# The first eight rows of x loaded by SyncE without a cast, and a kernel's prologue dealt out anew over the engines

## The chip, the cores and the metric

The kernel runs on one core of one Trainium2 chip. The metric is the time of one execution on the device in microseconds (us), as the median of several runs. The engines are named as in the profile: PE is TensorE, DVE is VectorE, ACT is ScalarE, POOL is GpSimd, SP is SyncE. In every trace of this case each of them works through its own instructions in the order of the program, and that order is what this study is about.

## The reference, cut to what matters

```python
def _attn_ref(x):                        # x: 8 x 3008 x 256, float32
    X = np.fft.fft(x, axis=1)
    X = np.fft.fft(X, axis=2)
    return X.real.astype(np.float32)

def _moe_ref(x, w_gate, w_val, w_out):   # 24064 tokens, 256 -> 1536 -> 256
    gate = np.maximum(x @ w_gate, 0.0)
    val = x @ w_val
    return (gate * val @ w_out).astype(np.float32)
```

The kernel does the Fourier transforms as matmuls with tables of cosines and sines, which it makes on the chip, and folds the last step of the transform into the two weight matrices. So before the main loop can start, a prologue has to load the first batch of x and the weights, make the tables, run the first transform stage, and fold the weights. The main loop begins with the first matmul into a tile called `G`.

## The kernel before: the parts that the change touches

GpSimd loads the first batch in pieces; the loads cast float32 to bfloat16 on the way. Rows 0 to 15 land in a tile `lo`, rows 16 to 31 in `hi` (through an index, in turned order).

```python
def load_first(r, n):
    # ... cut: makes the tile lo or hi at the first use
    if r < NB // 2:
        nc.gpsimd.dma_start(out=dst, in_=view(x, r * D, [[NB * D, 96], [1, n * D]]))
    else:
        # ... cut: indirect load of the same size on GpSimd

def ends(r, n):       # VectorE, a few columns
def back(r, n, evac): # a copy of the rows in reversed order, on ScalarE or VectorE
```

The weights come in halves of 128 rows; a pair is added and subtracted, and TensorE folds the sum and the difference with a cosine (`cs` 0) or sine table. The fold is in float32, on 64 columns of the array for each half.

```python
def pair_w(n, i, eng, parts=(0, 1)):
    lo, hi, up = (wst[i, n, c] for c in range(3))
    if 0 in parts: eng.tensor_tensor(up, lo, hi, op=ALU.add)         # L323
    if 1 in parts: eng.tensor_tensor(lo, lo, hi, op=ALU.subtract)    # L325

def fold_w(n, i, cs, ps=None):
    for k, w in ((0, wst[i, n, 2]), (1, wst[i, n, 0])):
        nc.tensor.matmul(ps[64 * k:64 * k + 64, :], lhsT=cd[:, cs, 64 * k:64 * k + 64], rhs=w, ...)  # L335
```

GpSimd's order before (cuts marked); the schedule is manual, so program order is the order on each engine:

```python
load_first(0, 8)
# ... cut: iotas for the row index ixf
load_first(24, 8); pl.iota(pi[:], ...); load_first(8, 4); load_first(20, 4)
# ... cut: two iotas
load_first(12, 4); load_first(16, 4)
pl.tensor_scalar(perm[:], dd[:], ...)
# ... cut: three iotas
load_w(0, pl)                            # four loads of the first weights
# tis: two 128x128 steps that need small columns from VectorE
# ... cut: di, s, rot
pair_w(0, 1, pl)                         # sum and difference of the value weights
```

VectorE makes the tables, the reversed copies, seven small column operations (`col`, 128x1 each), a masking step on `tis`, and then `pair_w(0, 0, dve)` for the gate weights. TensorE then runs: first stage, gate folds, two "upright" groups, value folds, first `G`.

## Time and profile before

| of the kernel before | value |
|---|---|
| time, median of 3 runs | 623.52 us (623.28 to 623.77) |
| span of the profiled run | 622.2 us |
| first matmul into G | 21.87 us |
| span after that point | 600.3 us |
| GpSimd's value sum begins, its difference ends | 16.43, 19.18 us |
| VectorE's gate sum begins | 15.12 us |
| TensorE's granted clock in the prologue | 1.00 |

Of 622 us, the change touches only the first 22. The prediction below shows the lines; a line of a timeline gives start, length, engine, source line, operation, tiles and shapes, and in brackets the idle time before it and what ended it.

### The profile page before, as it was taken

The page shows a single profiled execution, that of the slowest core. Times are in us where ns is not written, and L with a number is a line of the kernel's source. Part 1 is how long each engine was busy: PE and PEld are TensorE (multiplying, and loading weights), DVE is VectorE, ACT ScalarE, POOL GpSimd, SP SyncE. Part 2 cuts the span into 40 slices and gives each one's busy share as a digit, 9 for nine tenths or more (in the row PEclk, how much of TensorE's full clock was granted, in tenths as well). Part 3 has the DMA queues.
Part 4 walks back from the last instruction along what each step waited for, and adds up shares of the span by engine and source line. Part 5 has one row for each costly group of instructions (what it writes and reads, how often), then busy time and mean ns, then how long its engine had stood idle before and what let it go on. Part 6 is the DMA issues. An engine that isn't in the chain of part 4 may idle for free.

```text
span 622.2 us, 11959 instructions
## 1 busy us (share of the span) xinstructions
PE 613.3 (99%) x4284; PEld 409.1 (66%) x4284; DVE 537.0 (86%) x652; ACT 444.9 (72%) x855; POOL 519.9 (84%) x447
## 2 busy tenths in 40 slices
PE   8999999999999999999999999999999999999996
PEld 5346666666666666666667666666666666666665
DVE  7678998899888898898988998898988888899991
ACT  7677777777777777767777777767677676766661
POOL 8998998998898898899988998888988965555665
PEclk9999999999999999999999999999999999999998
DMA  8994283425462182613843255531822134112114
GB/s 168 243 166 111 84 217 89 112 66 177 111 154 61 47 220 87 149 36 95 211 107 89 67 164 123 141 75 34 234 71 58 34 85 125 52 34 67 34 35 100
DMA packets 42038, 67.44 MB, mean 108 GB/s; under 512 B 5877, under 2 KB 31774, under 8 KB 39962
## 3 DMA queue, kind: packets, MB, share of 16 engines
q1 hardware_dynamic: 37162, 50.61, 31.5%
q0 software_dynamic: 4656, 15.88, 10.8%
q8 instruction: 33, 0.54, 0.4%
q10 hardware_dynamic: 160, 0.20, 0.1%
q14 instruction: 27, 0.22, 0.1%
HBM read 38.85 MB, written 30.17 MB: 111 GB/s over the span
## 4 chain that ended last, share of the span: by engine, by line
PE 96%; DMA 1%; POOL 1%; DVE 1%; issue 0%; ACT 0%; POOLq 0%
PE po L686 40%; PE V L636 20%; PE G L620 10%; PE G L621 10%; PE G L627 10%; PE psw L335 2%; PE ps L164 2%; PE ps L273 2%; DMA lo<-in_x_dram 1%; POOL hi L133 0%; PE pst L242 0%; PE ps L218 0%; PE ps L168 0%; DVE E L643 0%; POOL lo L130 0%
## 5 line engine op out<-in xcount | busy, mean ns | idle before, releaser
L657 POOL TENSOR_TENSOR h<-gm,E 128x992 bf16<-128x992 f32 (+1 forms) x138 | 319.9, 2318 | 82.0 <-DVE E L664 52.9
L686 PE MATMUL po<-wo,h 128*128 128x256 bf16 (+2 forms) x2304 | 328.5, 272 | 0.0
L686 PEld LDWEIGHTS <-h 128*128 128x128 bf16 (+2 forms) x2304 | 231.3, 103 | 106.0 <-issue 0.2
L629 ACT ACTIVATE gm<-G 128x496 f32<-128x496 f32 (+1 forms) x288 | 170.4, 592 | 94.4 <-PE G L627 87.2
L650 DVE TENSOR_TENSOR h<-gs,V 128x1024 bf16<-128x1024 f32 (+3 forms) x150 | 173.8, 1159 | 62.1 <-PE V L636 42.1
L643 DVE SCALAR_TENSOR_TENSOR E<-nb,af,V 128x496 f32<-128x496 bf16 (+1 forms) x276 | 190.1, 730 | 1.1 <-PE V L636 0.7
L622 ACT ACTIVATE gs<-G 128x497 f32<-128x497 f32 (+2 forms) x288 | 169.7, 589 | 24.6 <-PE G L621 24.4
L664 DVE SCALAR_TENSOR_TENSOR E<-E,V 128x992 f32<-128x992 f32 (+1 forms) x138 | 164.3, 1191 | 0.0
L620 PE MATMUL G<-pq,wc 128*128 128x497 bf16 (+2 forms) x288 | 108.0, 375 | 0.0
L621 PE MATMUL G<-pq,ws 128*128 128x497 bf16 (+2 forms) x288 | 108.0, 375 | 0.0
L627 PE MATMUL G<-pq,wm 128*128 128x496 bf16 (+1 forms) x288 | 107.9, 375 | 0.0
L636 PE MATMUL V<-pq,wc 128*128 128x497 bf16 (+2 forms) x288 | 85.5, 375 | 0.3 <-DVE h L657 0.3
L636 PE MATMUL V<-pq,ws 128*128 128x497 bf16 (+2 forms) x288 | 85.4, 375 | 0.2 <-DVE E L643 0.2
L621 PEld LDWEIGHTS <-ws 128*128 128x128 bf16 x288 | 28.2, 98 | 31.6
L699 ACT COPY os<-po 128x512 f32<-128x512 f32 x63 | 36.9, 586 | 14.3 <-PE po L686 12.0
L620 PEld LDWEIGHTS <-wc 128*128 128x128 bf16 x288 | 28.2, 98 | 20.1 <-issue 1.6
L115 POOL TENSOR_TENSOR eo<-xla 94x256 bf16<-94x256 f32 x56 | 40.5, 730 | 0.6
L636 PEld LDWEIGHTS <-wc 128*128 128x128 bf16 x288 | 28.2, 98 | 19.0 <-issue 0.5
L115 POOL TENSOR_TENSOR eo<-xlb 94x256 bf16<-94x256 f32 (+1 forms) x42 | 34.4, 820 | 0.7
L112 POOL TENSOR_TENSOR xla<-xla,xha 94x510 f32<-94x510 f32 x28 | 32.9, 1174 | 2.2
L179 ACT CAST t<-ps 96x512 bf16<-96x512 f32 x56 | 32.7, 584 | 2.3 <-PE ps L164 0.2
L627 PEld LDWEIGHTS <-wm 128*128 128x128 bf16 x288 | 28.1, 98 | 3.8
(140 smaller groups left out, 366.2 us busy)
## 6 DMA issues: line engine op xcount, KB each, us to landing
out_dram<-os SPq DMA_DIRECT2D x124, 128.0 KB
Td<-t SPq DMA_DIRECT2D x7, 768.0 KB
t<-Td SPq DMA_DIRECT2D x7, 768.0 KB
out_dram<-os SPq DMA_DIRECT2D x82, 64.0 KB
xla<-in_x_dram SPq DMA_DIRECT2D x7, 720.0 KB
xlb<-in_x_dram SPq DMA_DIRECT2D x6, 640.0 KB
nb<-Nd SPq DMA_DIRECT2D x23, 128.0 KB
out_dram<-os SPq DMA_DIRECT2D x40, 48.0 KB
```

The lines of the kernel that those rows point to most:

```text
L115: yield eng.tensor_tensor(e1[:, :, k:k + H], x1[:, :, 0:H], free(x1, D, [DX, n], [-1, H]), op=op)
L620: nc.tensor.matmul(G[:, ds], lhsT=wc[0][:, fs], rhs=pq[:, 0, ds], start=True, stop=False)
L621: nc.tensor.matmul(G[:, ds], lhsT=ws[0][:, fs], rhs=pq[:, 1, ds], start=False, stop=True)
L622: nc.scalar.activation(pair(t, "gs")[:, t % 2, ds], G[:, ds], ACTF.Relu)
L627: nc.tensor.matmul(G[:, cols], lhsT=wm[0][:, f * 128:(f + 1) * 128], rhs=pqt[b, blk][:, 1, cols], start=False, stop=True, skip_group_check ...
L629: nc.scalar.activation(pair(t, "gm")[:, t % 2, cols], G[:, cols], ACTF.Relu)
L636: nc.tensor.matmul(o, lhsT=w[:, f * 128:(f + 1) * 128], rhs=pqt[b, blk][:, min(k, 1), cs], start=(k == 0), stop=(k > 0 or split(t)), skip_ ...
L643: nc.vector.scalar_tensor_tensor(pair(t, "E")[:, t % 2, cols], nbt[b, blk][:, cols], af[:, f:f + 1], pair(t, "V")[:, t % 2, cols], op0=ALU ...
L650: nc.vector.tensor_tensor(pair(t, "h")[:, k, 0, 0:ds.stop - ds.start], pair(t, "gs")[:, k, ds], val, op=ALU.mult)
L657: eng.tensor_tensor(free(pair(t, "h")[:], 1024 * (t % 2) + 512 + w - 1, [1024, n], [-1, w]), pair(t, "gm")[:, k, cols], val[:, :, cols], o ...
L664: nc.vector.scalar_tensor_tensor(E[:, :, cols], E[:, :, cols], 2.0, V[:, :, cols], op0=ALU.mult, op1=ALU.subtract)
L686: nc.tensor.matmul(po[0:m, i, :], lhsT=pair(t - f + ff, "h")[:, ff % 2, sg, g * 128:g * 128 + m], rhs=wo[:, ff, :], start=(ff == 0), stop= ...
```

## The change

Its intent: SyncE is idle at the start and can issue a load at once, but in this kernel only GpSimd issues casting loads. So SyncE loads rows 0 to 7 as float32 into a tile of batch 1 that is not used yet (`x8`), and copies on GpSimd cast them into `lo`, which the first matmuls read. That frees one issue on GpSimd and lets the stream of transfers begin sooner. VectorE's reversed copies read `x8` directly; two new copies on GpSimd (the "casts") make rows 0 to 7 of `lo`. Small work is dealt out otherwise: the columns to GpSimd, one negation from ScalarE to VectorE, one evacuation from VectorE to ScalarE, perm and some iotas behind the weight loads.

```diff
+        x8 = tabs["x8"] = x_tile(False, 0)
+        nc.sync.dma_start(out=x8[:, 0:8, :], in_=view(x, 0, [[NB * D, 96], [1, 8 * D]]))
 ...
-        load_first(0, 8)
 ...
         load_first(8, 4)
+        pl.tensor_copy(xt[0]["lo"][0:NA, 2:8, 0:H], x8[0:NA, 2:8, 0:H])      # 1st cast
         load_first(20, 4)
 ...
-        pl.tensor_scalar(perm[:], dd[:], ...)
+        pl.iota(pi[:], ...)
+        pl.tensor_copy(xt[0]["lo"][0:NA, 0:2, 0:H], x8[0:NA, 0:2, 0:H])      # 2nd cast
+        load_w(0, pl)
         # ... three iotas
-        load_w(0, pl)
 ...
         def col(tag, a, *args, **kw):
-            dve.tensor_scalar(t[:], a[:], *args, **kw)
+            pl.tensor_scalar(t[:], a[:], *args, **kw)
 ...
-        warm(9)
+        warm(4)
-        nc.scalar.mul(wn[:, 0, 9:16, :], wn[:, 1, 9:16, :], -1.0)
+        dve.tensor_scalar(wn[:, 0, 9:16, :], wn[:, 1, 9:16, :], scalar1=-1.0, ...)
 ...     # VectorE's angle, bits and table steps for cd stand later
+        pl.tensor_scalar(perm[:], dd[:], ...)
 ...
+        dve.tensor_scalar(tis[:], tis[:], scalar1=NB - 1, ..., op0=ALU.bitwise_and)
         pair_w(0, 0, dve)
-        first_evac(0, "dve")
+        first_evac(0, "act")
```

More of the change, by code (lines that the diff above doesn't have):

```diff
@@ L185, in ends @@
     def ends(r, n):
-        v = xt[0]["lo" if r < NB // 2 else "hi"][0:NA, r % 16:r % 16 + n, :]
+        v = (tabs["x8"] if r < 8 else xt[0]["lo" if r < NB // 2 else "hi"])[0:NA, r % 16:r % 16 + n, :]
         if r < NB // 2:
@@ L196, in back @@
         dst = tabs["back"][:, r:r + n, 1:H]
-        src = free(xt[0]["lo" if r < NB // 2 else "hi"][0:NA], r % 16 * D + D - 1, [D, n], [-1, H - 1])
+        src = free((tabs["x8"] if r < 8 else xt[0]["lo" if r < NB // 2 else "hi"])[0:NA], r % 16 * D + D - 1, [D, n], [-1, H - 1])
         if evac == "act":
@@ L409 @@
         load_first(24, 8)
-        pl.iota(pi[:], pattern=[[0, 1]], base=0, channel_multiplier=1)
         load_first(8, 4)
+        pl.tensor_copy(xt[0]["lo"][0:NA, 2:8, 0:H], x8[0:NA, 2:8, 0:H])
         load_first(20, 4)
@@ L416 @@
         load_first(16, 4)
-        pl.tensor_scalar(perm[:], dd[:], scalar1=mi[:], scalar2=None, op0=ALU.is_equal)
+        pl.iota(pi[:], pattern=[[0, 1]], base=0, channel_multiplier=1)
+        pl.tensor_copy(xt[0]["lo"][0:NA, 0:2, 0:H], x8[0:NA, 0:2, 0:H])
+        load_w(0, pl)
         iota(pl, ui[:], [[1, 4], [0, NB]], 0, 0)
@@ L466 @@
             sines(free(wz[:], 192 * (k + 1), [97, 2], [2, 48]), both[0], S, 2.0 * k - 1.0)
-        nc.scalar.mul(wn[:, 0, 9:16, :], wn[:, 1, 9:16, :], -1.0)
-        back(0, 2, "dve")
-        dve.tensor_scalar(da[:], dd[:], scalar1=mi[:], scalar2=None, op0=ALU.mult)
-        residue(da[:], dq[:], D, dve)
-        absolute(dq[:], da[:])
-        cosines(cd[:, 0, 1:H], dq[:, 1:H], D)
-        sines(cd[:, 1, 1:H], da[:, 1:H], D, 1.0)
-        jj, sl, up, odd = bits(0, 15), bits(4, 1), bits(5, 3), bits(0, 1)
+        dve.tensor_scalar(wn[:, 0, 9:16, :], wn[:, 1, 9:16, :], scalar1=-1.0, scalar2=None, op0=ALU.mult)
         ends(24, 8)
@@ L483 @@
         back(8, 4, "act")
+        dve.tensor_scalar(da[:], dd[:], scalar1=mi[:], scalar2=None, op0=ALU.mult)
+        residue(da[:], dq[:], D, dve)
         for c in (1, 2, 3):
             first_evac(c, "act")
+        absolute(dq[:], da[:])
+        cosines(cd[:, 0, 1:H], dq[:, 1:H], D)
+        sines(cd[:, 1, 1:H], da[:, 1:H], D, 1.0)
+        jj, sl, up, odd = bits(0, 15), bits(4, 1), bits(5, 3), bits(0, 1)
         z = col("z", jj, scalar1=0.0, scalar2=None, op0=ALU.is_equal)
@@ L498 @@
             pl.tensor_scalar(ti[cs], kbi[:], scalar1=mul[:], scalar2=(o0, o1)[cs][:], op0=ALU.mult, op1=ALU.add)
-        dve.tensor_scalar(tabs["wzn"][:], wz[:, 0], scalar1=-1.0, scalar2=None, op0=ALU.mult)
-        dve.tensor_copy(cd[:, 1, 0:1], odd[:])
-        dve.tensor_scalar(cd[:, 0, 0:1], odd[:], scalar1=-1.0, scalar2=1.0, op0=ALU.mult, op1=ALU.add)
-        dve.tensor_scalar(ui[:], ui[:], scalar1=up[:], scalar2=-1.0, op0=ALU.is_equal, op1=ALU.mult)
         group((4, 5), False)
@@ L508 @@
         group((4, 5), True)
+        dve.tensor_scalar(tabs["wzn"][:], wz[:, 0], scalar1=-1.0, scalar2=None, op0=ALU.mult)
+        back(0, 2, "dve")
         ends(12, 4)
@@ L512 @@
         back(16, 4, "dve")
-        dve.tensor_scalar(tis[:], tis[:], scalar1=NB - 1, scalar2=None, op0=ALU.bitwise_and)
+        dve.tensor_copy(cd[:, 1, 0:1], odd[:])
+        dve.tensor_scalar(cd[:, 0, 0:1], odd[:], scalar1=-1.0, scalar2=1.0, op0=ALU.mult, op1=ALU.add)
+        dve.tensor_scalar(ui[:], ui[:], scalar1=up[:], scalar2=-1.0, op0=ALU.is_equal, op1=ALU.mult)
+        pl.tensor_scalar(perm[:], dd[:], scalar1=mi[:], scalar2=None, op0=ALU.is_equal)
         group((6, 7, 0), False)
@@ L520 @@
         first_evac(5, "act")
+        dve.tensor_scalar(tis[:], tis[:], scalar1=NB - 1, scalar2=None, op0=ALU.bitwise_and)
         pair_w(0, 0, dve)
-        for cs in range(2):
-            nc.scalar.activation(sv[cs][:], ti[cs], ACTF.Sin, scale=2.0 * math.pi / NB * (1.0 - 2e-7), bias=npi[:])
         group((6, 7, 0), True)
@@ L526 @@
         first_evac(7, "act")
-        first_evac(0, "dve")
+        first_evac(0, "act")
+        for cs in range(2):
+            nc.scalar.activation(sv[cs][:], ti[cs], ACTF.Sin, scale=2.0 * math.pi / NB * (1.0 - 2e-7), bias=npi[:])
         for cs in range(2):
```

## The prediction

> **What bounds the kernel now.** I read the page first: busy shares, then the chain that ended last.
>
> ```profile
> span 622.2 us, 11959 instructions
> PE 613.3 (99%) x4284; PEld 409.1 (66%) x4284; DVE 537.0 (86%) x652; ACT 444.9 (72%) x855; POOL 519.9 (84%) x447
> PE 96%; DMA 1%; POOL 1%; DVE 1%; issue 0%; ACT 0%; POOLq 0%
> ```
>
> TensorE is the bound for nearly the whole span. The main loop begins at 21.87 us (first matmul into G); after that its waits add up to less than 1 us. The change touches only instructions before that point, so the question is: when does the first G matmul start in the changed kernel? A shift there passes to the end nearly one to one, since later waits are too small to absorb it.
>
> I then read the DMA share in stretches (columns: stretch, busy time of PE, PEld, DVE, ACT, POOL, granted clock, DMA share, GB/s as written):
>
> ```profile
> 2.00:2.60 0.60, 0.60 (x3) 0.17 (x2) 0.56 (x2) 0.22 (x2) 0.49 (x4) 1.00 0.00 0
> 2.60:4.00 1.40, 1.40 (x5) 0.56 (x4) 1.33 (x4) 0.64 (x2) 1.11 (x2) 1.00 0.88 105
> 4.00:6.00 2.00, 1.67 (x8) 0.46 (x6) 1.92 (x6) 1.68 (x4) 1.70 (x4) 1.00 1.05 176
> 12.00:15.00 3.00, 2.54 (x29) 1.97 (x27) 1.79 (x8) 1.65 (x4) 2.58 (x7) 1.00 0.94 326
> 15.00:16.00 1.00, 1.00 (x13) 0.84 (x12) 0.84 (x2) 0.89 (x4) 0.00 (x0) 1.00 0.17 66
> ```
>
> The DMA engines are empty until 2.6, slow until 4.0, then full until about 15. So x and the first weights arrive at the pace of the transfers, and an earlier start is worth having. Last, the timeline of GpSimd, and of TensorE around the end of the prologue (start, length, then the idle time before and its releaser):
>
> ```profile
> 1.40 0.66 POOL L130 DMA_DIRECT2D lo<-in_x_dram  x1 [0.22 <-issue]
> 3.04 1.19 POOL L133 DMA_INDIRECT hi<-in_x_dram,ixf  x1 [0.29 <-POOL ixf L408]
> 11.76 1.13 POOL L498 TENSOR_SCALAR tis<-kbi,t 128x128 int32<-128x128 f32 x2
> 13.12 0.25 POOL L532 TENSOR_SCALAR s<-mi 128x1 f32<-128x1 f32 x1
> 14.38 0.41 POOL L537 TENSOR_SCALAR rot<-di 128x8 bf16<-128x8 f32 x1
> 16.43 1.27 POOL L323 TENSOR_TENSOR wst<-wst 128x512 f32<-128x512 f32 x1 [1.64 <-DMA wst<-in_moe_w_val_dram]
> 17.78 1.40 POOL L325 TENSOR_TENSOR wst<-wst 128x512 f32<-128x512 f32 x1
> ```
>
> ```profile
> 15.87 1.80 PE L335 MATMUL psw<-wst,cd 128*64 128x512 f32 x4
> 19.52 1.08 PE L335 MATMUL psw<-wst,cd 128*64 128x512 f32 x4
> 21.87 0.38 PE L620 MATMUL G<-pq,wc 128*128 128x496 bf16 x1
> ```
>
> GpSimd is almost without a pause from 0.85 to 14.79, waits 1.64 us for the value weights, and then adds and subtracts them until 19.18. The TensorE matmuls at 19.52 read exactly that pair. GpSimd's only slack is this 1.64 us plus under 1 us behind the subtraction.
>
> **What the Trainium skill says.** "DMA: Bandwidth & Descriptors", section "SWDGE vs HWDGE vs iDMA": a DMA that casts must be issued from GpSimd. This is why the new SyncE load must stay uncast and a compute engine must cast. The trace agrees as far as it goes: every cast load of x and of w_out is on GpSimd. Same page, "Issuing engines are not separate DMA queues": issuing from another engine saves issue time, not bandwidth. Here one issue on GpSimd takes 0.66 us, and the engines behind are at full share, so I count no bandwidth won. Same page, "Latency and other measured facts": first byte after 0.6 us from SyncE and 1 us from GpSimd. The trace shows longer for both: 1.40 to 2.6, thus 1.2 us, on GpSimd; and 14.69 (SyncE's first weight load) to 16.0, where the emptied engines begin again, thus 1.3 us. "GPSIMD Engine Reference", § 4.1 Engine selection: one-input operations are roughly line-rate on GpSimd, two-input ones about twice as slow as VectorE. The two-input side agrees (1270 against 693 ns for 128x512); no one-input operation of some length is in the trace.
>
> **The change part by part.**
>
> 1. *SyncE loads rows 0 to 7 (786 KB, fp32).* SyncE is free from about 0.75. With 1.3 us to first movement, transfers start near 2.1 instead of 2.6. A transfer of equal size and row length on SyncE's queue, the transposed intermediate's write, lands 3.9 us after its issue (27.6 us of waits over 7) plus 0.31 for the issue. So x8 lands about 0.75 + 4.2 = 5.0; the indirect load of rows 24 to 31, now issued near 2.2, shares the engines from about 3.4 on, so I take 5.2. Before, the cast rows arrived at 5.98. The stream as a whole gains about 0.5 us of start and 0.5 us of ramp: 1 us.
>
> 2. *GpSimd casts.* 94x6x128, then 94x2x128. The trace's two-input slope is (1174-209)/(510-4) = 1.9 ns per element; the skill's line rate would be under 1 ns. Estimate 1.2 ns plus 0.2 fixed: 1.1 us for 768 elements and 0.5 us for 256. GpSimd reaches the first copy after iotas, ixf, the indirect load and the 4-row load, near 4.0, waits until 5.2, and is done at 6.3. The first products need this, so they begin at 6.3 instead of 5.98; VectorE's reversed copy reads x8 directly and is ready earlier. This is not the bound.
>
> 3. *Seven 128x1 column operations move from VectorE to GpSimd.* On VectorE about 0.17 each. On GpSimd the comparable row (s, 128x1) takes 0.25, and most wait for the one before, about 0.08 more: 7 x 0.32 = 2.2 us.
>
> 4. *GpSimd loses* the 0.66 us load issue. Its iotas and perm move, without changing their sum; but perm and three iotas now lie behind the weight issues.
>
> The GpSimd chain: from the end of the first copy (6.3), the stretch that before ran from 4.92 to 8.31 (two indirect loads, one load, two iotas; 3.4 us), the pi iota and second copy (0.7), four weight issues (2.28): 12.7. Then iotas 0.5, columns 2.2, tis 1.1, perm 0.5, di, s and rot 1.9: 18.9. Then the addition and subtraction, 2.75: 21.6. Before this was 19.18, so +2.5 us. The values of w_val would be there by about 16, so the wait for DMA is gone; GpSimd's own queue takes its place.
>
> 5. *VectorE and ScalarE.* VectorE loses the columns (1.2 us) and takes the wn negation (0.34) off ScalarE (0.75). The evacuation of group 0 goes from VectorE (0.55 + 0.56) to ScalarE. But VectorE's bitwise step on tis stands ahead of its sum of the gate weights; tis is done on GpSimd near 16.4, so that sum starts about 16.8 instead of 15.12, and the first weight fold on TensorE near 17.5 instead of 15.87. This +1.6 lies beside item 4's delay, not on top: TensorE then has about 3 us of work before the fold that needs the subtraction.
>
> 6. *TensorE* runs 5 fewer warm-up matmuls (5 x 0.23 us), in a wait for data: no gain.
>
> On the path: the fold at 19.52 has its second half at about 20.06, against a subtraction done at 19.18, so 0.88 us of the 2.5 is slack. First G matmul: 21.87 + 2.5 - 0.88 = 23.5, thus +1.6 us. All of part 1's DMA gain is hidden behind this.
>
> **The rivals.** (a) The DMA stream sets the end: all of x and the first weights come 1 us earlier and GpSimd keeps up. For it: the engines are full from 4 to 15, and someone tuned this order by hand. Against: the GpSimd sum, with only 1.64 us of slack. If each GpSimd piece is at its lower end (x8 at 4.5, copies 0.8 and 0.4, columns 0.25), the chain shrinks by about 1.6 us, and the whole is level; a gain of 1 us (622.5) needs still more. (b) TensorE's clock drops. "TensorE: Matmul & The Clock Gate", Part 1: an idle window of about 3.4 us halves the clock. If TensorE idles near 3 us ahead of the first fold, the fp32 folds could run at half rate and add 1 to 2 us: 626 to 627. The trace of before shows a granted clock of 1.00 throughout the prologue, with no such idle time, so it can neither support nor refute this. (c) The copy of 768 elements costs the two-input slope (1.7 us) and blocks against VectorE: another +0.6 us to 1 us.
>
> **Range and chances.** My sum gives 623.5 + 1.6 = 625.1. As rival (a) weighs more than (b) and (c) together, I shade it to 624.8. The range goes from the DMA gain (622.4) to clock loss on top of the GpSimd delay (627.0). All of this is within 0.6%, and 2% is 12.5 us, as much as half the prologue; so within 2% is nearly certain.
>
> **What would show it.** In the changed profile: x8 landing (GpSimd's wait before the first copy) near 5.2; that copy near 1.1 us; the columns near 0.3 each; no wait for w_val before GpSimd's addition, which starts near 18.9; VectorE's gate sum released by tis; first G matmul near 23.5; span near 624. I am wrong if GpSimd's addition still waits for the DMA, if it starts before 17.5, or if the first G matmul comes before 21.9. If the start of G and the span shift by different amounts, my step that carries the shift to the end is wrong.

## The result, and the profile after

The changed kernel took 627.87 us (median of 4 runs, 627.17 to 628.41) against 623.58 us for the kernel before on the same chip. The ratio is 1.0069 (95% interval 1.0051 to 1.0086). The change made the kernel 0.7% slower. That is within 2%, but outside the predicted range of 622.4 to 627.0.

From the page of the changed kernel (span; busy time, share and instructions of each engine; the chain that ended last, by engine):

```profile
span 626.5 us, 11918 instructions
...
PE 612.3 (98%) x4247; PEld 409.5 (65%) x4279; DVE 535.4 (85%) x644; ACT 445.6 (71%) x856; POOL 522.3 (83%) x455
...
PE 95%; POOL 2%; DMA 1%; issue 1%; DVE 1%; ACT 0%; POOLq 0%
```

TensorE still fills the span; only GpSimd's part of the chain has grown, from 1% to 2%. The timeline of GpSimd in the changed kernel:

```profile
6.49 0.83 POOL L412 CAST lo<-xha 94x768 bf16<-94x768 f32 x1 [2.52 <-DMA xha<-in_x_dram]
7.49 1.07 POOL L133 DMA_INDIRECT hi<-in_x_dram,ixf  x1 [0.17 <-issue]
...
10.82 0.39 POOL L419 CAST lo<-xha 94x256 bf16<-94x256 f32 x1
11.16 1.15 POOL L317 DMA_DIRECT2D wst<-in_moe_w_gate_dram  x2
...
13.97 0.28 POOL L447 TENSOR_SCALAR t<-tf 128x1 f32<-128x1 f32 x1
...
16.53 0.87 POOL L499 TENSOR_SCALAR tis<-kbi,t 128x128 int32<-128x128 f32 x2
...
20.22 1.27 POOL L323 TENSOR_TENSOR wst<-wst 128x512 f32<-128x512 f32 x1
21.57 1.27 POOL L325 TENSOR_TENSOR wst<-wst 128x512 f32<-128x512 f32 x1
```

GpSimd stands still for 2.52 us until `x8` has landed. Only then does it issue its next load, at 7.49. The weights are issued at 11.16 instead of 9.44. The columns take from 13.97 to 16.43. The value sum, which before waited 1.64 us for its data, now starts at 20.22 with no wait at all: the queue is the bound. VectorE and TensorE of the changed kernel:

```profile
17.44 0.46 DVE L522 TENSOR_SCALAR tis<-tis 128x256 int32<-128x256 int32 x1 [2.28 <-POOL tis L499]
17.82 0.68 DVE L323 TENSOR_TENSOR wst<-wst 128x512 f32<-128x512 f32 x1
```

```profile
18.55 2.70 PE L335 MATMUL psw<-wst,cd 128*64 128x512 f32 x4 [2.67 <-DVE wst L323]
21.18 1.03 PE L242 MATMUL pst<-perm,t 128*128 128x128 bf16 x8
...
23.63 1.08 PE L335 MATMUL psw<-wst,cd 128*64 128x512 f32 x4
...
25.98 0.38 PE L622 MATMUL G<-pq,wc 128*128 128x496 bf16 x1
```

VectorE's gate sum is held behind `tis`, and so behind GpSimd. TensorE is idle for 2.67 us ahead of the first fold. That fold then takes 2.70 us instead of 1.80, and the upright groups take 1.03 instead of 0.62. The stretches of the changed kernel show why (columns as in the prediction's table of stretches: the stretch and its length, then PE, PEld, DVE, ACT, POOL, granted clock, DMA share, GB/s):

```profile
2.00:2.60 0.60, 0.60 (x3) 0.18 (x2) 0.56 (x2) 0.21 (x2) 0.38 (x1) 1.00 0.39 96
2.60:4.00 1.40, 1.40 (x5) 0.57 (x4) 1.33 (x4) 0.63 (x2) 1.38 (x2) 1.00 1.03 310
...
8.20:8.60 0.40, 0.40 (x7) 0.28 (x5) 0.40 (x3) 0.25 (x2) 0.39 (x2) 1.00 0.00 0
8.60:9.00 0.40, 0.40 (x3) 0.19 (x2) 0.22 (x4) 0.37 (x1) 0.40 (x3) 1.00 0.00 0
...
18.00:20.00 2.00, 1.45 (x3) 0.48 (x4) 1.62 (x4) 0.62 (x2) 1.81 (x5) 0.75 0.83 283
20.00:22.00 2.00, 2.00 (x11) 0.77 (x8) 0.00 (x0) 0.71 (x2) 1.91 (x3) 0.50 1.00 352
```

Three things are to be seen. The stream does begin sooner, as was intended: a DMA share of 0.39 between 2.0 and 2.6, where it was 0.00. (The 310 GB/s between 2.6 and 4.0, instead of 105, say less: bytes are counted as written, and `x8` is written as float32, the casting loads as bfloat16.) But it stands empty from 8.2 to 9.0, because GpSimd issued nothing between 3.98 and 7.49; the early start is given back there. And the granted clock falls to 0.50 after TensorE's idle time. Rows 0 to 7 themselves came no sooner: the first products, which need them, began at 5.98 before and begin at 7.38 now.

The first `G` moved from 21.87 to 25.98 us, by 4.1 us; the span after it is 626.5 - 25.98 = 600.5 us, against 600.3 before. So all but 0.2 us of the loss is made in the prologue.

### The profile page after: what moved, and what is told of

Its sections match the earlier page's. It is cut to its first block, busy times and chain, and to the rows that moved or that the text cites. A ratio compares the mean times of both kernels' runs of the same rounds, so it can differ in the third digit from the quotient of the medians.

```text
span 626.5 us, 11918 instructions
## 1 busy us (share of the span) xinstructions
PE 612.3 (98%) x4247; PEld 409.5 (65%) x4279; DVE 535.4 (85%) x644; ACT 445.6 (71%) x856; POOL 522.3 (83%) x455
## 4 chain that ended last, share of the span: by engine, by line
PE 95%; POOL 2%; DMA 1%; issue 1%; DVE 1%; ACT 0%; POOLq 0%
PE po L688 40%; PE V L638 19%; PE G L622 10%; PE G L629 10%; PE G L623 10%; PE psw L335 2%; PE ps L164 2%; PE ps L273 2%; DMA xha<-in_x_dram 1%; PE pst L242 0%; POOL wst L317 0%; POOL hi L133 0%; POOL t L447 0%; PE ps L168 0%; DVE E L645 0%
## 5 line engine op out<-in xcount | busy, mean ns | idle before, releaser
L622 PE MATMUL G<-pq,wc 128*128 128x496 bf16 (+2 forms) x287 | 107.6, 375 | 1.1
L623 PE MATMUL G<-pq,ws 128*128 128x496 bf16 (+2 forms) x287 | 107.6, 375 | 0.1
L638 PE MATMUL V<-pq,ws 128*128 128x496 bf16 (+2 forms) x280 | 83.7, 374 | 0.2 <-DVE E L645 0.2
L638 PE MATMUL V<-pq,wc 128*128 128x496 bf16 (+2 forms) x267 | 80.9, 374 | 0.3 <-DVE h L659 0.3
L638 PEld LDWEIGHTS <-wc 128*128 128x128 bf16 x288 | 28.2, 98 | 18.9 <-issue 0.5
```

Source lines behind the costliest of these rows:

```text
L622: nc.tensor.matmul(G[:, ds], lhsT=wc[0][:, fs], rhs=pq[:, 0, ds], start=True, stop=False)
L623: nc.tensor.matmul(G[:, ds], lhsT=ws[0][:, fs], rhs=pq[:, 1, ds], start=False, stop=True)
L638: nc.tensor.matmul(o, lhsT=w[:, f * 128:(f + 1) * 128], rhs=pqt[b, blk][:, min(k, 1), cs], start=(k == 0), stop=(k > 0 or split(t)), skip_ ...
```

## The experiments

All twelve kernels below gave correct results. The kernel before took 623.43 to 623.78 us (median) in each of the groups of runs.

### Half of the change at a time

**The load alone.** The kernel before with SyncE's load and the two casts on GpSimd, nothing else moved.

```diff
 (against the kernel before)
+        x8 = tabs["x8"] = x_tile(False, 0); nc.sync.dma_start(out=x8[:, 0:8, :], ...)
-        load_first(0, 8)
+        pl.tensor_copy(xt[0]["lo"][0:NA, 2:8, 0:H], x8[0:NA, 2:8, 0:H])   # behind load_first(8, 4)
+        pl.tensor_copy(xt[0]["lo"][0:NA, 0:2, 0:H], x8[0:NA, 0:2, 0:H])   # behind load_first(16, 4)
         # ends() and back() read x8 for rows 0 to 7
```

> The kernel before with the SyncE load of x and the two GpSimd casts alone; nothing else is dealt out otherwise. Theory: GpSimd waits for the load until 6.4, casts, and issues the rest about 2.2 us later than before; its sum of the value weights starts near 18.4 instead of 16.43, first G near 22.9, so 1 us slower than before, 624.6, with the clock at 1.00. Rival (the load by itself is the whole loss): 627 to 628. Rival (the load helps and only the dealing-out hurts): 622.5 to 623.

Measured: 626.12 us (5 runs, 625.16 to 626.43), ratio 1.0033 (1.0020 to 1.0047); first `G` at 24.07. The load by itself costs 2.2 us in the prologue, and the expected 624.6 was missed. GpSimd's difference ended at 21.67.

**The deal alone**, that is, the small work dealt out anew. The changed kernel with GpSimd's casting load back and neither `x8` nor the casts.

```diff
 (against the changed kernel)
-        x8 = ...; nc.sync.dma_start(out=x8[:, 0:8, :], ...)
+        load_first(0, 8)
-        pl.tensor_copy(..., x8[0:NA, 2:8, 0:H])
-        pl.tensor_copy(..., x8[0:NA, 0:2, 0:H])
```

> The changed kernel with the cast load of rows 0 to 7 back on GpSimd at its old place and without x8 and the casts: the dealing-out alone. Theory: GpSimd's weight issues end near 10.8, the columns cost 2.5 us, tis is done near 14.7, about when the gate weights land, and the sum of the value weights starts near 17.5 instead of 16.43; most of this is slack: 0.2 to 0.9 us slower than before, 623.8 to 624.5, clock 1.00. Then the two parts' losses (1.0 and 0.2 to 0.9) add up to less than half of the 4.3 us, and the rest comes from their meeting on one queue and from the clock. Rival (the parts simply add): 626 to 627 here if the load alone is worth 1.

Measured: 625.06 us (5 runs, 624.78 to 625.43), ratio 1.0021 (1.0008 to 1.0035); first `G` at 22.83, GpSimd's difference ended at 20.44. The deal alone costs 1.0 us in the prologue, and each half of the change loses time. Together they would make 2.2 + 1.0 = 3.2 us; the whole change made 4.1. So they nearly add, and there is a rest of 0.9 us, to which the lost clock of the changed kernel's trace belongs. In the median times the rest is smaller: 2.5 + 1.4 = 3.9 of 4.3 us. The expectation, that the two would make less than half of the loss, was wrong, and so was its time of 623.8 to 624.5.

**The columns back on VectorE.** One word of the changed kernel.

```diff
-            pl.tensor_scalar(t[:], a[:], *args, **kw)
+            dve.tensor_scalar(t[:], a[:], *args, **kw)
```

> The changed kernel with the seven 128x1 column operations back on VectorE, all else kept. Theory (GpSimd's queue is the bound of the prologue): GpSimd loses the stretch from 13.97 to 16.43, 2.46 us; tis is done near 15.0, VectorE's gate sum starts near 16 (then held by the landing of the gate weights), TensorE idles under 1.5 us before the first fold, the granted clock stays at 1.00, GpSimd's addition starts near 17.8 and the first G matmul near 22.5: about 3.5 us less than the changed kernel's 627.9, so 624.4. Rival (the late landing of x on SyncE's queue is the cause): the landing at 6.4 is untouched, so at most 0.5 us is won, 627.4. Rival (the halved clock alone is the cause, worth about 1 us): 626.9 at best.

Measured: 625.89 us (5 runs, 625.64 to 627.63), ratio 1.0046 (1.0032 to 1.0060); first `G` at 23.47 in the profiled run. This one word takes back 2.0 us of the loss of 4.3 in the median, 1.4 us in the mean of the runs. The expected 624.4 was missed. The five runs fall in two kinds: three of 625.6 to 625.9 with a mean granted clock of 0.997 to 0.999, and two of 627.2 and 627.6 with 0.992. The columns are not the whole cause: the wait for `x8` and the casts stay on GpSimd.

### Is it VectorE's order and TensorE's clock, or GpSimd's queue?

**The gate sum ahead of the tis step.** This removes TensorE's idle time before the first fold, and with it the drop of the clock. A theory that puts the loss on the clock expects a gain; a theory that puts it on GpSimd's queue expects the wait to come back at the value fold.

```diff
-        dve.tensor_scalar(tis[:], tis[:], ..., op0=ALU.bitwise_and)
         pair_w(0, 0, dve)
+        dve.tensor_scalar(tis[:], tis[:], ..., op0=ALU.bitwise_and)
```

> The changed kernel with VectorE's sum of the gate weights ahead of its bitwise step on tis (two lines exchanged). Theory: the sum starts when the gate weights land, near 16, the first fold on TensorE near 16.8 instead of 18.55, and the granted clock stays at 1.00; but the fold that needs GpSimd's subtraction still waits for it until 22.84, so the first G matmul comes near 24.9 instead of 25.98: 1.1 us won, 626.8. Rival (VectorE's order, with the clock loss that it causes, is the whole cause): 624 or less. Rival (order is harmless): 627.9.

Measured: 628.04 us (5 runs, 627.41 to 628.53), ratio 1.0069 (1.0055 to 1.0083): nothing won. TensorE in this kernel:

```profile
21.48 1.07 PE L335 MATMUL psw<-wst,cd 128*64 128x512 f32 x2 [0.78 <-POOL wst L323]
22.83 1.07 PE L335 MATMUL psw<-wst,cd 128*64 128x512 f32 x2 [0.27 <-POOL wst L325]
...
25.17 0.38 PE L622 MATMUL G<-pq,wc 128*128 128x496 bf16 x1
```

The first fold began at 16.78, and the clock stayed at 1.00 through the prologue. But TensorE then waited for GpSimd's sum and again for its difference, and `G` came only 0.8 us sooner than in the changed kernel's trace; the median shows not even that. So GpSimd's queue is the bound, and the lost clock lies mostly beside it. The lines also show a length that the prediction had wrong: two of these matmuls take 1.07 us, and four take 1.08 (the line at 23.63 above). The two halves of a fold run side by side. The second half is therefore not a tail of 0.54 us: whoever comes last for it is followed by 1.07 us of fold.

**The first cast behind all loads of x.** If the blocked queue is the cost, moving the cast behind the loads should start loads, weights and columns sooner.

```diff
         load_first(8, 4)
-        pl.tensor_copy(..., x8[0:NA, 2:8, 0:H])
         load_first(20, 4)
 ...
         pl.iota(pi[:], ...)
+        pl.tensor_copy(..., x8[0:NA, 2:8, 0:H])
         pl.tensor_copy(..., x8[0:NA, 0:2, 0:H])
```

> The changed kernel with GpSimd's first cast moved behind all its loads of x, so that GpSimd's wait for x8 holds back no DMA issue. Theory (the wait stands in an in-order queue ahead of the issues): the DMA engines no longer stand idle between 8.0 and 9.2, the weight issues begin near 8.8 instead of 11.16, the subtraction of the value weights ends near 20.5 instead of 22.84, and the first G matmul follows 2.4 us later, near 22.9: 624.7. The columns still cost their 2.5 us, so it stays above the kernel before. Rival (the wait for x8 is harmless, only the columns and casts count): 627 to 628.

Measured: 626.85 us (4 runs, 625.44 to 627.22), ratio 1.0042 (1.0027 to 1.0058). The GpSimd side came as expected: the weights were issued from 8.87, and the difference ended at 20.70, 2.1 us sooner than in the changed kernel. But another wait took the place, and the expected 624.7 was missed. TensorE in this kernel, and one stretch of it:

```profile
8.63 1.14 PE L218 MATMUL ps<-wn,lo 94*128 94x192 bf16 x6 [2.98 <-POOL lo L418]
```

```profile
10.00:12.00 2.00, 2.00 (x9) 1.09 (x8) 1.79 (x15) 0.00 (x0) 2.00 (x7) 0.50 0.89 221
```

The first products need the cast rows, and got them at 8.63. TensorE had been idle for 2.98 us, the clock fell to 0.50, and the six products took 1.14 us instead of 0.67. The one run with a mean clock of 0.998 took 625.44. Here the clock is a real cost, because the matmuls at half rate lie on the path: the first fold began only when the first stage was over, at 19.14.

**Both casts on VectorE.** The load stays, and GpSimd neither waits for it nor casts.

```diff
-        pl.tensor_copy(..., x8[0:NA, 2:8, 0:H])
-        pl.tensor_copy(..., x8[0:NA, 0:2, 0:H])
 ...
         ends(0, 8)
+        dve.tensor_copy(..., x8[0:NA, 2:8, 0:H])
 ...
+        dve.tensor_copy(..., x8[0:NA, 0:2, 0:H])
         back(0, 2, "dve")
```

> The changed kernel with both casts on VectorE instead of GpSimd; GpSimd then never waits for x8 at all. Theory: weight issues begin near 7.6; but the columns on GpSimd need VectorE's bit fields, which are done near 12, so that the columns end near 14.6 and the subtraction near 21: first G near 23.2, 624.9. So the columns alone keep most of the loss, as in the run of the dealing-out alone (625.1). Rival (without GpSimd's wait for x8 all of the loss is gone): 623.6 or less.

Measured: 624.67 us (4 runs, 624.53 to 624.85), ratio 1.0016 (1.0000 to 1.0031). This is 3.2 us less than the changed kernel: the casts and the wait on GpSimd are most of the loss. It is also 0.4 us less than the change without the load (625.06), with `G` 0.5 us sooner, so the early load no longer costs anything; whether it gains, these two intervals, which overlap, do not settle. In this kernel GpSimd issued the weights at 7.70, its difference began at 18.62 and ended at 19.89, and `G` came at 22.29, that is 2.40 us later. In three of the versions above (the load alone, the deal alone, the gate sum first) the same distance is 24.07 - 21.67, 22.83 - 20.44 and 25.17 - 22.77: again 2.4 us. VectorE's reversed copy of 94x762 took 0.55 us here and 1.19 in the changed kernel, where it ran beside GpSimd's cast.

### Why x8 came late

**x8 with nothing of GpSimd's in flight.** GpSimd casts before it issues any load of its own. This is slow on purpose; it tells whether x8 came late because it shared the engines.

```diff
+        xt.setdefault(0, {})["lo"] = tp.tile([96, J, D], BF16, tag="eo", name="lo")
+        pl.tensor_copy(..., x8[0:NA, 2:8, 0:H])
         load_first(24, 8)
         load_first(8, 4)
-        pl.tensor_copy(..., x8[0:NA, 2:8, 0:H])
```

> A measurement of the load, not a better kernel: GpSimd casts x8 before it issues any of its own loads, so SyncE's load has the DMA engines to itself. If sharing with GpSimd's loads makes x8 late, it lands near 5.0 (the 4.2 us of an equal transfer on this queue after an issue at 0.75) instead of 6.1 to 6.6. If the path itself is slow, it lands at 6 again. The kernel as a whole is slower than the changed one either way (about 629), since every load of GpSimd starts later.

Measured: one look, 630.4 us (a single run, so its state isn't known). GpSimd in this kernel, and two stretches of it:

```profile
5.92 0.83 POOL L411 CAST lo<-xha 94x768 bf16<-94x768 f32 x1 [3.99 <-DMA xha<-in_x_dram]
```

```profile
4.00:5.00 1.00, 1.00 (x4) 0.29 (x2) 0.93 (x3) 1.00 (x2) 0.00 (x0) 1.00 0.68 180
5.00:6.00 1.00, 0.90 (x4) 0.20 (x2) 0.77 (x5) 0.93 (x3) 0.08 (x1) 1.00 0.01 0
```

Even alone, the load released the cast only at 5.92. It was issued at 0.74, the first bytes moved at about 1.6, the last before 4.8, and 1.1 us more went by until GpSimd could go on. So the transfer itself needs 5.2 us from its issue. In the other kernels with this load VectorE got x8 between 6.0 and 6.8, against 5.9 here, so sharing adds 0.1 to 0.9 us, as far as one look tells.

### Is there a version that beats both?

**Casts and columns on VectorE, perm and rot early on GpSimd.** GpSimd's small steps then lie in the time in which it waited for the weights.

```diff
 (against the version with both casts on VectorE)
-            pl.tensor_scalar(t[:], a[:], *args, **kw)      # col
+            dve.tensor_scalar(t[:], a[:], *args, **kw)
 # perm, di, s and rot: from behind tis to right behind load_w(0, pl) and its iotas
```

> A version meant to beat both: the SyncE load kept, the casts and the columns on VectorE, and GpSimd's perm, di, s and rot ahead of tis, so that GpSimd neither waits for x8 nor has work left when the value weights land. Theory: the DMA stream is 1 us earlier than in the kernel before, the value weights land near 15.4, the subtraction ends near 18.2, the last rows of x land near 12.9, the first fold starts near 15, and the first G comes near 20.9: 622.7, 1 us faster than before. Rival (the uncast load costs as much as it gains; it lands later than the cast load did and shares the same engines): 623.6 or more.

Measured: 624.52 us (5 runs, 624.38 to 625.23), ratio 1.0015 (1.0002 to 1.0029); the expected 622.7 was missed. GpSimd and TensorE in this kernel:

```profile
15.03 1.55 POOL L323 TENSOR_TENSOR wst<-wst 128x512 f32<-128x512 f32 x1 [0.93 <-DMA wst<-in_moe_w_val_dram]
```

```profile
13.01 0.42 PE L218 MATMUL ps<-wn,hi 94*128 94x192 bf16 x3 [1.42 <-DVE hi L192]
...
22.45 0.38 PE L621 MATMUL G<-pq,wc 128*128 128x496 bf16 x1
```

The value sum waits for its data again and begins 1.4 us sooner than before the change: the intent of the change, the earlier stream, is there. GpSimd's difference ended at 18.26, which would allow `G` at 20.7. But VectorE now has the columns and the casts, and TensorE waits 1.42 us for rows 20 to 23, whose handling stands behind them. The gain went into VectorE's queue.

**Rows 20 to 23 first.** VectorE handles these rows ahead of the residue, bits and columns, and makes the gate sum ahead of two small table steps (`ui`, `tis`).

```diff
+        ends(20, 4); back(20, 4, "dve")       # moved up, ahead of:
         dve.tensor_scalar(da[:], dd[:], ...)  # residue, bits, columns
 ...
-        dve.tensor_scalar(ui[:], ...); dve.tensor_scalar(tis[:], ...)
         pair_w(0, 0, dve)
+        dve.tensor_scalar(ui[:], ...); dve.tensor_scalar(tis[:], ...)
```

> As the version with the casts and columns on VectorE and GpSimd's perm and rot early (624.5 us), but VectorE's handling of rows 20 to 23 stands ahead of the residue, bits and columns (it stood behind, and TensorE waited 1.42 us for it), and its sum of the gate weights stands ahead of the last two small table steps (0.5 us earlier). If VectorE's queue is what ate the DMA gain: no wait of over 0.7 us on TensorE between 9 and 16, the first fold starts near 15.3 instead of 16.09, the gate subtraction ends near 16.6 instead of 17.13, the first G matmul near 21.5 instead of 22.45, and the time is 623.3 us (level with before or just under it). Rival: the rows of the later loads arrive no sooner, so TensorE waits for the same transfer elsewhere, the first G matmul stays at 22.3 to 22.6, and the time stays at 624.5. Other rival: the columns end later and GpSimd's tis, then its addition of the value weights, slip past 15.5; then the subtraction ends near 19 and G starts near 21.5 to 22.

Measured: 626.39 us (5 runs, 625.89 to 627.44), ratio 1.0046 (1.0032 to 1.0060): a clear miss, 1.9 us worse. TensorE in this kernel, and a stretch of it:

```profile
14.40 0.26 PE L218 MATMUL ps<-wz,lo 94*128 94x192 bf16 x1 [2.12 <-DVE lo L513]
```

```profile
16.00:17.00 1.00, 1.00 (x9) 0.95 (x8) 1.00 (x1) 0.17 (x1) 1.00 (x1) 0.50 0.96 342
```

VectorE waited 0.79 us for those rows at its new place, and the cast of rows 0 and 1 now stood behind everything. TensorE's wait moved there and grew to 2.12 us, after which the clock fell to 0.50.

**The gate sum first, and nothing else.** The second half of that edit alone.

```diff
 (against the version with casts and columns on VectorE)
-        dve.tensor_scalar(ui[:], ...); dve.tensor_scalar(tis[:], ...)
         pair_w(0, 0, dve)
+        dve.tensor_scalar(ui[:], ...); dve.tensor_scalar(tis[:], ...)
```

> As the version of 624.5 us (casts and columns on VectorE, perm and rot early), with one move: VectorE's sum of the gate weights ahead of two small table steps (0.55 us). If the end of that pair's subtraction, 17.13, is what holds the first fold's second half: the sum starts at 14.25 and the subtraction ends at 16.2 to 16.5, the fold is over at 17.3 to 17.6 instead of 18.25, G starts at 21.6 to 21.9, time 623.8 us. Rival: the gate weights land only at 14.7, or the subtraction is stretched more beside GpSimd's addition: G stays at 22.3, time 624.4.

Measured: 624.03 us (5 runs, 623.69 to 625.06), ratio 1.0014 (1.0001 to 1.0028), `G` at 21.77. That is within what was expected for `G`, and 0.5 us better than with the old order in the median. But two of the five runs were at 624.8 and 625.1, and the ratios to the kernel before, 1.0014 here and 1.0015 with the old order, do not tell the two apart; so a gain in time is not shown.

**Rows 20 to 23 between the bits and the columns.** The same, with `ends(20, 4)` and `back(20, 4, "dve")` in the middle of VectorE's block.

```diff
         jj, sl, up, odd = bits(0, 15), bits(4, 1), bits(5, 3), bits(0, 1)
+        ends(20, 4); back(20, 4, "dve")
         z = col("z", jj, ...)                 # and the other columns
 ...
-        ends(20, 4); back(20, 4, "dve")
```

> The same, and VectorE's handling of rows 20 to 23 between the bits and the columns, not behind them (the run before this put it ahead of both and everything else behind, and that moved TensorE's wait to the cast of rows 0 and 1). TensorE's one wait of 1.42 us becomes two shorter ones (about 0.5 at rows 20 to 23 and about 0.6 at the cast of rows 0 and 1), stage 1 ends near 15.5, the fold is over at 17.0 to 17.3, G at 21.3 to 21.6, time 623.2 to 623.5 us. Rival: VectorE's queue is full, and what is moved ahead delays the cast of rows 0 and 1 as much as it saves: stage 1 ends at 16.0 to 16.3 again, and the time is that of the other run, 623.8.

Measured: 623.92 us (5 runs, 623.65 to 624.09), ratio 1.0005 (0.9992 to 1.0019). This is level with the kernel before, the best of the versions with the new load, and 0.4 to 0.7 us above what was expected. TensorE in this kernel:

```profile
13.05 0.26 PE L218 MATMUL ps<-wz,lo 94*128 94x192 bf16 x1 [0.47 <-DVE lo L513]
...
19.01 0.17 PE L261 MATMUL psr<-t,rot 128*128 128x4 bf16 x1 [0.86 <-DVE t L248]
...
21.70 0.38 PE L621 MATMUL G<-pq,wc 128*128 128x496 bf16 x1
```

The wait was split as planned, and the first fold began at 15.04. But a new wait of 0.86 us stood at 19.01. VectorE's `ui` step, now behind the gate sum, ran beside GpSimd's value sum and took 1.29 us, and what TensorE needed stood behind it.

**ui ahead of the gate sum.** One step of that version moved back.

```diff
+        dve.tensor_scalar(ui[:], ...)
         pair_w(0, 0, dve)
-        dve.tensor_scalar(ui[:], ...)
         dve.tensor_scalar(tis[:], ...)
```

> As the version that was level with before (623.92 us), with one step (ui, 128x128) ahead of VectorE's sum of the gate weights. There it stood behind that sum and took 1.29 us beside GpSimd's addition, and TensorE then waited 0.86 us for VectorE's cast behind it. Ahead of the sum it should take 0.27. If that step is what holds the end of the prologue: TensorE's wait of 0.86 us shrinks to 0.3 or less, G starts at 21.0 to 21.3 instead of 21.70, and the time is 623.2 to 623.5 us, 0.3 to 0.6 us under before at best. Rival: the gate sum starts 0.2 later and its subtraction is stretched beside GpSimd's addition instead, as it was (1.65 us) in the first of these versions: the fold is over 0.5 later, G stays at 21.6 to 22.0, time 623.9.

Measured: 624.23 us (5 runs, 623.71 to 625.43), ratio 1.0014 (1.0001 to 1.0028); nothing won. VectorE in this kernel:

```profile
14.53 0.27 DVE L528 TENSOR_SCALAR ui<-ui,tf 128x128 f32<-128x128 f32 x1
...
16.04 1.37 DVE L530 TENSOR_SCALAR tis<-tis 128x256 int32<-128x256 int32 x1
```

`ui` took 0.27 us as expected. Then `tis`, which had taken 0.28 in the version before, stood in its place and took 1.37. TensorE's wait shrank only from 0.86 to 0.71 us. In this run the value weights also came at least 0.6 us later, so part of the miss may be that. None of the versions beat the kernel before.

## Why the prediction was right or wrong

The direction was right: a loss, at the place named, by the mechanism named. The size was not: 624.8 was predicted, 627.87 measured.

- *"GpSimd's own queue takes its place"* (right). The value sum has no wait for data in the changed kernel. Taking the casts off GpSimd gave back 3.2 us, and taking the columns off 2.0 us. Together that is more than the loss of 4.3, so the two can't be added: both shorten the same queue, and in the version with both on VectorE it was VectorE's queue that came last.
- *x8 "lands about 0.75 + 4.2 = 5.0 ... so I take 5.2"* (this step failed). It landed at 6.43. The transfers began sooner than predicted, at 1.6 and not 2.1; it is the transfer that is longer. The 4.2 us came from a write to memory of equal size in the main loop; the load needs 5.2 us from its issue even when it is alone. This made GpSimd's end later by 1.2 us. Beside this, the prediction did not draw a consequence: while GpSimd waits, it issues nothing, and the transfers ran dry from 8.2 to 9.0.
- *Copies, 1.1 and 0.5 us* (too high): 0.83 and 0.39, so 0.4 us less together. Of rival (c) the slow copy falls. Its blocking against VectorE did come: VectorE's reversed copy took 1.19 us and ended at 7.73, after the cast (7.32) and not before it as predicted. But the products that read it began at 7.88, after those that read the cast, so it did not set the time.
- *Columns, 2.2 us* (near): 2.46. The steps di, s and rot took 2.2 instead of 1.9.
- *Addition at 18.9, difference at 21.6*: 20.22 and 22.84. The delay is the late x8 (+1.2), columns and rot (+0.6), and faster copies and issues (-0.5 or so).
- *VectorE's gate sum held by tis, near 16.8, and the first fold near 17.5, "beside item 4's delay, not on top"* (right, both 1.0 us too early): 17.82 and 18.55, late by what GpSimd was late. That it lies beside is shown by the run with the gate sum first: the fold came 1.8 us sooner, and the median stayed.
- *"0.88 us of the 2.5 is slack"* (this step failed too). The prediction took the second half of a fold to be half of its time. The halves run side by side, and a late half takes its full 1.07 us. With nothing else in the way, `G` follows the difference by 2.40 us; in the kernel before this was 21.87 - 19.18 = 2.69. So the slack was 0.3.
- *Rival (b), a lost clock after "near 3 us" of idle time* (it came in this trace, and should have been in the sum). TensorE was idle for 2.67 us, and the clock fell to 0.50. `G` came 25.98 - 22.84 = 3.14 us after the difference, 0.74 more than 2.40.

The three terms make up the miss at `G`: 1.24 (GpSimd's end) + 0.58 (slack) + 0.74 (clock) = 2.56 us, against 25.98 - 23.5 = 2.48; the rest is rounding in the prediction. The miss in the time is larger, 627.87 - 624.8 = 3.1 us. Of this, 0.3 us come from shading 625.1 down to 624.8 for rival (a), the gain by transfers, which did not happen; the last 0.3 are the 0.2 us after `G` and the difference between medians and profiled runs.

- *"A shift there passes to the end nearly one to one"* (right). The span after the first `G` is 600.3 us before, 600.5 after, and 600.1 to 600.7 in the twelve experiments, with `G` anywhere from 21.70 to 27.89.
- *TensorE's five fewer warm-up matmuls: no gain*: not tested apart, and neither were the negation and the evacuation that changed engines.
- *The gain of the stream, "hidden behind this"* (right, and shown): where neither casts nor columns were on GpSimd, the value weights were there 1.4 us sooner. But only by giving that work to VectorE, which was full as well.

What stays open: how often the clock falls in the timed runs. Each kernel has one trace. The record gives the mean clock of every timed run: of the changed kernel's four, two at 0.995 and 0.994 took 628.3 and 628.4 us, and two at 0.997 and 0.999 took 627.2 and 627.4. So the profiled run, at 0.995, is one of the slower two, and a lost clock may cost about 1 us in half of the runs. But the version without idle time ahead of the first fold had a full clock in its trace and yet the same median as the changed kernel, with its slowest run, 628.53, at 0.998. So the 0.74 us is shown for one execution and not for the median.

## What to carry to other kernels

When you give an engine a step that waits for a transfer, count all that stands behind it in its queue, above all its own issues of later transfers: here a wait of 2.5 us held back loads, weights and the last sum alike. Before you hand work to an engine "with slack", reckon its slack up to the moment at which the consumer really needs the result, with the consumer's whole length behind it, and not a part of it. In this prologue, where GpSimd and VectorE were both nearly full, moving small steps mostly moved the wait: four reorderings of VectorE's queue came out, in medians, between 0.6 us better and 1.9 us worse than the order they started from, and none beat the original kernel.

## What the Trainium skill lacked or had wrong

- "DMA: Bandwidth & Descriptors", section "Latency and other measured facts": first byte after 0.6 us from SyncE. Here the load was issued at 0.74, and the first bytes moved at about 1.6, so 0.9 us after the issue began and 0.5 us after it had ended (it took 0.39); the runs don't contradict the page. The page's fixed cost of about 2 us agrees with 0.9 + 1.1 us (first bytes, and last bytes to the released cast). What the section lacks is a transfer time by size for a load from SyncE: in the one look, alone, 786 KB needed 3.2 us between first and last bytes.
- "TensorE: Matmul & The Clock Gate", Part 1: an idle window of about 3.4 us lowers the clock. Here, in one trace of each kernel, the clock fell to 0.50 after idle times of 2.12, 2.67, 2.98 and 3.96 us, and stayed at 1.00 after 1.15, 1.42 and 1.77 us. In this prologue, 2 us was already too long. In the same traces the clock came back 3.4 us (after 2.12 and 2.67) or 6.8 us (after 2.98 and 3.96) after it had fallen, so the page's length shows here as the length of the slow stretch.
- "GPSIMD Engine Reference", § 4.1 Engine selection: one-input operations are roughly line-rate. The casts agree: 0.83 us for 768 elements and 0.39 for 256, thus 0.86 ns for each element more; VectorE did the same casts in 0.55 and 0.28 us where nothing stretched them. But the chained 128x1 columns took 0.35 us each (2.46 us over 7) on GpSimd, against 0.18 on VectorE (1.25 over 7); the section has no figure for short operations.
- "SBUF — State Buffer", section "Who interferes with whom", treats VectorE and GpSimd getting in each other's way, so nothing is lacking there; these are the sizes. Beside a GpSimd cast or sum, VectorE took 1.19 us instead of 0.55 (cast, 94x762), 1.29 instead of 0.27 (128x128), and 1.37 instead of 0.28 (128x256). In these three VectorE's step ended 0.1 to 0.4 us after GpSimd's, as if it had stood and waited for it; no run tests that apart.
